# Scales from maxima, disjoint places, deferred loads and smaller pieces in a spectral feed-forward kernel

## The chip, the cores and the metric

The kernel runs on one core of one Trainium2 chip. The metric is the device time of one execution in microseconds (us), lower is better. Before the change it is 1247.22 us, the median of three runs (1246.28 to 1248.51). A core has five engines that work through their own instruction queues in order and wait for each other through semaphores: TensorE (PE in the profile; PEld is its loading of weights), VectorE (DVE), ScalarE (ACT), GpSimd (POOL) and SyncE (SP). DMAs are issued from the queues of SP, ACT and POOL, and stand in order with what else these queues hold.

## The reference

Inputs: x (2048 x 1024), complex filter weights w_r and w_i (2048 x 513), w1 (1024 x 3584) and w2 (3584 x 1024).

```
xn = layernorm(x)
s  = irfft2(rfft2(xn) * (w_r + 1j * w_i))
g  = silu(silu(xn @ w1) @ w2)
out = x + s * g
```

## The kernel before

**Precision.** Every matrix operand is split into two fp16 numbers, a high and a low part, scaled by powers of two; a product is three matmuls (high by high, high by low, low by high). A split costs one ScalarE activation (the high part, `high`, L232) and one VectorE operation (the low part, `low`, L235).

**First product.** xn is kept transposed in four row blocks c of 512 rows. w1 is taken in 28 column blocks f of 128. One call of `mm1(c, f)` is 24 matmuls (L454) into one of four PSUM tiles of the tag "ff"; there are 112 such calls. ScalarE applies the SiLU on evacuation (L463) into h32, and `hidden` forms differences (L492 to L497), splits them and stores them in DRAM over GpSimd's queue (L486).

**Scales of w1.** `weights1` loads a block (L252, SP's queue, buffers of the tag "w1"), and `maxi` gives one number for each partition: for blocks 0 to 3 the largest absolute value by VectorE (L256), for the others the sum of squares by ScalarE (L258), whose elementwise result is not needed and is written into place 3 of the tile scr. `scales` adds the numbers over the partitions with a matmul by ones into an "ff" tile (L239) and takes a power of two (L267 to L276). Then come the splits.

**Transform.** `fd_gen` does the forward transform of a row block: `fa_mat` (L769 to L771, 24 small products into one of two PSUM tiles of the tag "ft"), `fa_evac` (L777, L778 on ScalarE), butterflies on VectorE (L788 to L833), then a stage over rows with VectorE (L867, `radix4` at L219 to L222, L851), ScalarE (L848) and a store over GpSimd's queue (L852). After it `f_gen` applies the filter (matmuls at L975), and `i_gen` does the inverse for the row blocks in the order 1, 3, 0, 2 (`mat`, L1258; `mat2`, L1300; `bfly`). `load_i` (L1234) loads the operand zt of `mat`: 2 MB for a row block, from DRAM; for the three later row blocks it is called in the inverse of the block before, after its fourth `mat`. A small copy (L1244, ScalarE) writes one column into zt before `mat`.

**Maxima of filter and w2.** `wmax_gen` goes through the filter in 16 row blocks: two loads (L893, SP's queue, buffers "x", four of them), a maximum on VectorE (L898), and copies of its columns in another order on ScalarE (L901, L903) into two of the four places of scr, from which GpSimd's queue stores them to DRAM (L905). A block is used three steps after its load. `w2max_gen` does the like with 28 row blocks of w2: a load (L359), sums and differences on VectorE into places 0 to 2 in turn (L364), stored over GpSimd's queue (L365), and a sum of absolute values on ScalarE (L371), with place 3 for the unused result.

**Second product.** It is a product of 2 x 2 blocks with seven multiplications. Each of the seven has eight output groups j; one `mm2` is 42 matmuls of 512 columns (L532 to L534). The operand of the hidden layer is loaded again (ht, L513, SP's queue), two products ahead; the weights come through GpSimd's queue (L400) and are split on the way. Partial sums are read and written (pl, pd), and the last products apply the SiLU (L613), multiply by the transform's rows (L606), add x (L607) and store the output (L609). The very last one is done in two halves of 256 columns.

**Order.** Nothing is reordered by a compiler: the order in which the program emits instructions is the order on each engine. After each product `after` runs: `settle` gives out the next stage of the evacuation, `tick` runs what was deferred (`defer(n, fn)` runs fn n ticks later), and `work` gives out one step of the list wq (w1, later w2), one step of the list xq (filter maxima, then w2 maxima) and up to three steps of the list bg (layernorm, transform, inverse). The bg steps are paced by two sums of estimated costs, kept for every emitted instruction of VectorE and TensorE:

```
COST = {"DVE": ("dve", 0.07, 1.045e-3), "PE": ("pe", 0.0025, 0.4167e-3)}
...
clock["dve"] = max(clock["dve"], clock["pe"] - 1.0)
for _ in range(3):
    if clock["dve"] > clock["pe"] + lead[0] or hold[0] or slot(bg) == PAUSE:
        break
```

with a lead of 1 us (2 us in `f_gen`). The inverse's steps on bg wait for nothing else; `f_gen` starts when the xq list is done.

Of the kernel before, what the change touches and what calls it, by code (L numbers as in the profile page):

```python
# [10 lines left out]
F32 = mybir.dt.float32  # L11
# [13 lines left out]
SUMMED = (4, 5)  # L25
TURNED = (2, 3)
AT = (1, 0)
EXTRA = (4, 5, 6, 7, 20, 22, 24)


# [75 lines left out]
def spectral_ffn(ctx, tc, x, w_r, w_i, w1, w2, ca, kc, ci, tw, pm, out):  # L106
    nc = tc.nc
# [15 lines left out]
    pf = ctx.enter_context(tc.tile_pool(name="pf", bufs=4, space=PSUM))  # L123
# [28 lines left out]
    def defer(n, fn):  # L152
        deferred.append([n, fn])
# [74 lines left out]
    w2m = small("w2m", NFT)  # L228
# [13 lines left out]
    def weights1():  # L242

        raw = {}

        def load(i):  # L250
            raw[i] = fp.tile([128, 8, 128], F32, name=f"w1r{i}", tag="w1", bufs=7)
            nc.sync.dma_start(raw[i], w1v[:, :, i * 128:(i + 1) * 128])  # L252

        def maxi(i):
            if i < 4:
                nc.vector.tensor_reduce(m1[:, i:i + 1], raw[i], axis=AX.XY, op=OP.max, apply_absolute_value=True)  # L256
            else:
                nc.scalar.activation(A["scr"][:, 3].bitcast(mybir.dt.bfloat16), raw[i].rearrange("a b c -> a (b c)"), AF.Square, accum_out=m1[:, i:i + 1])  # L258

        def scales(i, k):  # L260
            sl = slice(i, i + k)
            ps = column_sums(f"s1_{i}", m1[:, sl], k)
            if i < 4:
                nc.vector.tensor_single_scalar(e1[:, sl].bitcast(I32), ps.bitcast(I32), 0x7F800000, op=OP.bitwise_and)
                nc.vector.tensor_single_scalar(e1[:, sl], e1[:, sl], 2.0**-100, op=OP.max)
            else:
                nc.vector.tensor_scalar(e1[:, sl].bitcast(I32), ps.bitcast(I32), 1, 0x7F800000, op0=OP.logical_shift_right, op1=OP.bitwise_and)  # L267
                nc.vector.tensor_scalar(e1[:, sl], e1[:, sl], 2.0**63, 2.0**-60, op0=OP.mult, op1=OP.max)
            nc.vector.reciprocal(r1[:, sl], e1[:, sl])
            nc.vector.tensor_single_scalar(rs[:, sl], r1[:, sl], 2.0**14, op=OP.mult)  # L270
            nc.vector.tensor_single_scalar(s1[:, sl], e1[:, sl], 2.0**-24, op=OP.mult)
            if (i + k) % 2 == 0:
                p = (i + k) // 2 - 1
                nc.vector.tensor_tensor(ep[:, p:p + 1], e1[:, 2 * p:2 * p + 1], e1[:, 2 * p + 1:2 * p + 2], op=OP.max)
                nc.vector.tensor_tensor(hs[:, p:p + 1], r1[:, 2 * p:2 * p + 1], r1[:, 2 * p + 1:2 * p + 2], op=OP.min)
                nc.vector.tensor_single_scalar(hs[:, p:p + 1], hs[:, p:p + 1], 2.0**7, op=OP.mult)  # L276

        new = {}

        def split(i):  # L280
            new[i] = fp.tile([128, 2, 8, 128], F16, name=f"w1_{i}", tag="w1", bufs=7)
            high(new[i][:, 0], raw[i], rs[:, i:i + 1])

        def rest(i):
            w1t[i] = w = new.pop(i)
            low(w[:, 1], raw.pop(i), rs[:, i:i + 1], w[:, 0])

        for i in range(4):
            load(i)
        yield 0  # L290
        maxi(0)
        yield 0
        maxi(1)
        yield 0
        scales(0, 2)
        yield 0
        split(0)
        rest(0)
        yield 0
        split(1)  # L300
        rest(1)
        maxi(2)
        maxi(3)
        yield 0
        scales(2, 2)
        split(2)
        rest(2)
        yield 2
        split(3)
        rest(3)  # L310
        yield 2
        def ahead(i):

            if i < NFT and i not in raw and i - len(used1) <= 4:
                load(i)
                load(i + 1)

        last = None
        for i in range(4, NFT, 2):
            while i not in raw:  # L320
                ahead(i)
                yield 0
                if last is not None:
                    rest(last)
                    last = None
            maxi(i)
            if last is not None:
                rest(last)
            yield 0
            maxi(i + 1)  # L330
            yield 0
            ahead(i + 2)
            yield 0
            ahead(i + 2)
            yield 0
            scales(i, 2)
            yield 0.8
            split(i)
            ahead(i + 2)
            yield 0.2  # L340
            rest(i)
            split(i + 1)
            ahead(i + 2)
            yield 0.2
            last = i + 1
        rest(last)
# [3 lines left out]
    def w2max_gen():  # L350

        ap = A["p"]
        scr = A["scr"]
        junk, slots = scr[:, 3].bitcast(F16), [0]
        tiles = {}
        for i in range(NFT + 3):
            if i < NFT:
                tiles[i] = ap.tile([128, 1024], F32, name=f"w2m{i}", tag="x", bufs=4)
                nc.sync.dma_start(tiles[i], w2[i * 128:(i + 1) * 128, :])  # L359
            if 3 <= i <= NFT + 2:  # L360
                def both(m, x0, x1, op):
                    d = scr[:, slots[0] % 3]
                    slots[0] += 1
                    nc.vector.tensor_tensor(d, x0, x1, op=op)  # L364
                    defer(1, lambda q=(i - 3) // 2: stores[0].dma_start(ws[m][q], d))  # L365

                t_ = tiles.pop(i - 3)
                if i % 2:
                    both(0, t_[:, 0:512], tiles[i - 2][:, 512:1024], OP.subtract)
                both(1 + i % 2, t_[:, 0:512], t_[:, 512:1024], OP.add)  # L370
                nc.scalar.activation(junk, t_, AF.Abs, accum_out=w2m[:, i - 3:i - 2])  # L371
            yield 0.7
        nc.vector.tensor_reduce(w2x, w2m, axis=AX.X, op=OP.max)
# [510 lines left out]
    def wmax_gen():  # L884

        ap = A["p"]
        scr = A["scr"]
        tl = {}
        for k in range(19):
            if k < 16:  # L890
                tl[k] = ap.tile([128, 2, 512], F32, name=f"wm{k}", tag="x", bufs=4)
                for i in range(2):
                    nc.sync.dma_start(tl[k][:, i], (w_r, w_i)[i][128 * k:128 * k + 128, 0:512])  # L893
            if k % 2:
                yield 0
            if k >= 3:
                t_, o = tl.pop(k - 3), scr[:, (slice(0, 2), slice(2, None, -2), slice(1, 3))[k % 3]]
                nc.vector.tensor_reduce(mt[:, k - 3:k - 2], t_, axis=AX.XY, op=OP.max, apply_absolute_value=True)  # L898
                src = t_.rearrange("m r (i l) -> m r l i", l=16)
                dst = o.rearrange("m r (g l i) -> m r l g i", g=4, l=4)  # L900
                nc.scalar.activation(o.rearrange("m r (l i) -> m r l i", i=32)[:, :, 0:4], src[:, :, 0:13:4], AF.Copy)  # L901
                for n, (la, st) in enumerate(((3, -1), (13, 1), (5, 1), (11, -1))):
                    nc.scalar.activation(dst[:, :, n, 1:4], src[:, :, la:la + 3 * st:st], AF.Copy)  # L903
                for i in range(2):
                    defer(1, lambda o=o, i=i, k=k: stores[0].dma_start(wp[i][128 * k - 384:128 * k - 256, :], o[:, i]))  # L905
            yield 1.1
# [329 lines left out]
    def i_gen(c):  # L1236
# [114 lines left out]
        for i in range(6):  # L1351
            if i < 4:
                mat(i)
            if i >= 2:
                split(i - 2)
            if 1 <= i <= 4:
                post(i - 1)
            yield PAUSE if i in (1, 2) else 3.9 if i in (3, 4) else 2
        if c != IORDER[-1]:
            n = IORDER[IORDER.index(c) + 1]  # L1360
            open_zt(n)
            load_i(n)
            load_kk(n)
        yield PAUSE
        for p in range(5):
            if p < 4:
                mat2(p)
            if p:
                bfly(p - 1)
            yield 3.4 if p else 0.3  # L1370
# [41 lines left out]
    with tc.manual_schedule():  # L1412
# [138 lines left out]
        for n, (m, j) in enumerate(seq):  # L1551
# [2 lines left out]
                    load_h(*seq[n + 2], k)  # L1554
            if n == len(seq) - 1:
                load_parts(m, j)
                for b in range(2):
                    cols = slice(256 * b, 256 * b + 256)
                    ps = pf.tile([128, 256], F32, name=f"pb{m}_{j}_{b}", tag="ff")
                    for k in range(2):  # L1560
                        mm2(m, j, ps, k, cols)
                    for _ in range(4 * b):
                        settle()
                        tick()
                    after(acc(m, j, ps, cols))
                break
# [54 lines left out]
```

## Time and profile before

| | |
|---|---|
| median of three runs | 1247.22 us (1246.28 to 1248.51) |
| the profiled execution, its own time | 1245.75 us |
| its span, first to last instruction | 1244.0 us |
| TensorE busy | 1209.3 us (97%) |
| VectorE busy | 1008.0 us (81%) |
| ScalarE busy | 524.2 us (42%) |
| GpSimd busy | 372.1 us (30%) |
| mean DMA rate over the span | 244 GB/s |

In a line of the profile, L454 is line 454 of the kernel, "pa<-xnT,w" says which tile is written from which, "x24" counts instructions, and in a timeline the bracket gives the idle time of the engine just before, and what ended it ("issue" where the profile shows nothing waited for). A wait for several semaphores is put down to the one that came last. Times are us from the span's start.

### The profile page before, as it was taken

Reading aid. Unit: us, or ns where it says so; the run is one execution under the profiler, and the core shown is the slowest. Engines: PE = TensorE matmul, PEld = TensorE weight load, DVE = VectorE, ACT = ScalarE, POOL = GpSimd, SP = SyncE. Lnnn points to the kernel's source line nnn. Section 1 sums busy time; section 2 is a strip of 40 time slices with the busy share of each in tenths; the row PEclk is TensorE's granted clock in tenths of the full one; section 3 lists DMA queues with packets and bytes.
Section 4 is the critical chain, followed back from the end, with each engine's and each line's share of the span. In section 5 each row is a group of like instructions: output and inputs, shape, how many; then the busy total and the mean of one; then the engine's idle time right before and its main releaser. Section 6 shows DMA issues by size and latency. Waiting matters only on the chain.

```text
span 1244.0 us, 21981 instructions
## 1 busy us (share of the span) xinstructions
PE 1209.3 (97%) x8335; PEld 602.4 (48%) x8335; DVE 1008.0 (81%) x2043; ACT 524.2 (42%) x716; POOL 372.1 (30%) x585
## 2 busy tenths in 40 slices
PE   7999999969999989999999999999999999999998
PEld 5544454435454434454444445445545544444544
DVE  6678998979989887549987998993876959779964
ACT  4865456847665565434444232121222212233221
POOL 1241153444453235313453224721212121010000
PEclk9999999999999999999999999999999999999999
DMA  7478477667687889565797989987877999994897
GB/s 239 124 177 200 127 257 226 211 221 222 227 300 226 280 280 292 173 189 153 218 319 217 295 240 273 275 252 215 213 235 220 272 341 298 288 390 176 274 372 264
DMA packets 170474, 303.79 MB, mean 244 GB/s; under 512 B 33584, under 2 KB 86480, under 8 KB 170368
## 3 DMA queue, kind: packets, MB, share of 16 engines
q1 hardware_dynamic: 131408, 183.48, 47.5%
q0 software_dynamic: 38816, 118.78, 31.7%
q8 instruction: 65, 1.06, 0.3%
q14 instruction: 41, 0.34, 0.1%
q10 hardware_dynamic: 144, 0.13, 0.0%
HBM read 185.39 MB, written 112.74 MB: 240 GB/s over the span
## 4 chain that ended last, share of the span: by engine, by line
PE 65%; DVE 6%; DMA 4%; ACT 1%; issue 1%; POOL 0%; SPq 0%; DVEq 0%; ACTq 0%; POOLq 0%
PE pa L454 22%; PE pb L532 13%; PE pb L534 12%; PE pb L533 12%; PE fx L975 2%; DMA ht<-hd_one 2%; PE iu L1258 1%; PE id L1300 1%; DMA vd<-Rs 1%; DMA ws<-scr 1%; DVE pl L606 0%; DVE scr L364 0%; DMA kv<-vd 0%; DVE hoone L235 0%; DVE us L1288 0%
## 5 line engine op out<-in xcount | busy, mean ns | idle before, releaser
L454 PE MATMUL pa<-xnT,w 128*128 128x512 f16 x2688 | 588.3, 380 | 7.1 <-ACT h L463 4.2
L454 PEld LDWEIGHTS <-w 128*128 128x128 f16 x2688 | 262.8, 98 | 320.8 <-issue 10.2
L532 PE MATMUL pb<-w,ht 128*128 128x512 f16 (+1 forms) x798 | 299.8, 376 | 1.8 <-DMA ht<-hd_one 1.8
L534 PE MATMUL pb<-w,ht 128*128 128x512 f16 (+1 forms) x798 | 299.5, 375 | 0.0
L533 PE MATMUL pb<-w,ht 128*128 128x512 f16 (+1 forms) x798 | 299.5, 375 | 0.0
L532 PEld LDWEIGHTS <-ht 128*128 128x128 f16 x798 | 78.0, 98 | 92.5 <-DMA ht<-hd_one 2.0
L534 PEld LDWEIGHTS <-ht 128*128 128x128 f16 x798 | 78.1, 98 | 91.2
L533 PEld LDWEIGHTS <-ht 128*128 128x128 f16 x798 | 78.1, 98 | 87.2
L463 ACT ACTIVATE h<-pa,s 128x512 f32<-128x512 f32 x112 | 75.7, 678 | 65.1 <-PE pa L454 57.9
L400 POOL DMA_DIRECT2D jr<-in_B_w_dram x56 | 35.2, 636 | 165.9 <-DVE w L235 47.4
L486 POOL DMA_DIRECT2D hd_sum<-hosum x52 | 38.5, 778 | 153.2 <-DVE hosum L235 77.6
L232 ACT ACTIVATE w<-jr,sc 128x512 f16<-128x512 f32 x98 | 67.9, 712 | 30.2 <-PE pb L534 16.3
L235 DVE SCALAR_TENSOR_TENSOR hoone<-h,hs,hoone 128x2048 f16<-128x2048 f32 x28 | 65.6, 2344 | 12.4 <-ACT hoone L232 6.6
L235 DVE SCALAR_TENSOR_TENSOR w<-jr,sc,w 128x512 f16<-128x512 f32 x98 | 71.6, 745 | 0.0
L232 ACT ACTIVATE hoone<-h,hs 128x2048 f16<-128x2048 f32 x28 | 55.9, 1996 | 28.2 <-DMA hd_one<-hoone 20.1
L492 DVE TENSOR_TENSOR hr<-h 128x1024 f32<-128x1024 f32 x28 | 34.2, 1220 | 35.2 <-ACT h L463 35.0
L486 POOL DMA_DIRECT2D hd_one<-hoone x52 | 46.1, 886 | 52.3 <-DVE hoone L235 29.7
L232 ACT ACTIVATE hosum<-hr,hs 128x1536 f16<-128x1536 f32 x28 | 44.0, 1572 | 41.5 <-DVE hr L493 35.5
L613 ACT ACTIVATE pl<-pl,c 128x512 f32<-128x512 f32 (+1 forms) x26 | 16.9, 683 | 102.0 <-DVE pl L592 53.3
L232 ACT ACTIVATE w<-w1r,rs 128x1024 f16<-128x1024 f32 x28 | 31.8, 1144 | 49.8 <-DVE w L235 37.7
L235 DVE SCALAR_TENSOR_TENSOR hosum<-hr,hs,hosum 128x1536 f16<-128x1536 f32 x28 | 50.7, 1812 | 1.1 <-ACT hosum L232 1.1
L365 POOL DMA_DIRECT2D ws<-scr x42 | 27.7, 678 | 51.7 <-DVE scr L364 42.5
(234 smaller groups left out, 1748.3 us busy)
## 6 DMA issues: line engine op xcount, KB each, us to landing
jr<-in_B_w_dram POOLq DMA_DIRECT2D x84, 256.0 KB, 7.2
w1r<-in_B_w_dram SPq DMA_DIRECT2D x28, 512.0 KB, 6.0
w2m<-in_B_w_dram SPq DMA_DIRECT2D x28, 512.0 KB, 6.5
ht<-hd_dif SPq DMA_DIRECT2D x32, 448.0 KB, 7.3
ht<-hd_sum SPq DMA_DIRECT2D x32, 448.0 KB, 5.7
ht<-hd_one SPq DMA_DIRECT2D x32, 448.0 KB, 8.2
hd_sum<-hosum POOLq DMA_DIRECT2D x52, 256.0 KB, 3.4
hd_one<-hoone POOLq DMA_DIRECT2D x52, 256.0 KB, 5.2
```

Source lines behind the costliest of these rows:

```text
L232: nc.scalar.activation(hi, raw, AF.Copy, scale=scale)
L235: nc.vector.scalar_tensor_tensor(lo, raw, scale, hi, op0=OP.mult, op1=OP.subtract)
L365: defer(1, lambda q=(i - 3) // 2: stores[0].dma_start(ws[m][q], d))
L400: nc.gpsimd.dma_start(raw[n], ws[m][q] if m in ws else w2_block(m, q, 0))
L454: nc.tensor.matmul(ps, w[:, wh, d], xt[:, xh, d], start=(n == 0), stop=(n == 23))
L463: nc.scalar.activation(hq[:, 2 * (c % 2) + f % 2], ps, AF.Silu, scale=s1[:, f:f + 1])
L486: defer(1, lambda k=k, m=m: stores[0].dma_start(hd[m, g][:, :, q].rearrange("f p h s -> f p (h s)"), o[:, k].rearrange("f p h s -> f p (h ...
L492: tt(sums[:, 0:2], hq[:, 0::2], hq[:, 1::2], op=OP.subtract)
L532: nc.tensor.matmul(ps, hh[:, 0], w[:, 0], start=first, stop=False)
L533: nc.tensor.matmul(ps, hh[:, 0], w[:, 1], start=False, stop=False)
L534: nc.tensor.matmul(ps, hh[:, 1], w[:, 0], start=False, stop=last)
L975: nc.tensor.matmul(o, k[rows_, h, e + 2 * x, kh, kind], B["v"][u, h][rows_, e + 2 * x, vh, cols], start=(n == 0 and kind == 1), stop=(n == ...
```

## The change

Five edits. (1) The column blocks 10 to 15 of w1 get their scale from the maximum on VectorE, as blocks 0 to 3 did; the sums of squares on ScalarE remain for the rest. (2) `wmax_gen` writes into places 0 and 1 and places 2 and 3 of scr in turn, in place of the three pairs (0, 1), (2, 0), (1, 2). (3) The loads of `wmax_gen` and `w2max_gen` are deferred by one tick. (4) For the three later row blocks of the inverse, `load_i` loads a quarter of zt at the old place and one more in each of the next three steps, ahead of the first three `mat2`. (5) The very last product is done in parts of 256, 128 and 128 columns.

```diff
+PEAKS = (0, 1, 2, 3, 10, 11, 12, 13, 14, 15)
...
         def maxi(i):
-            if i < 4:
+            if i in PEAKS:
...
         def scales(i, k):
...
-            if i < 4:
+            if i in PEAKS:
...
     def w2max_gen():
...
+        def load(i):
+            tiles[i] = ap.tile([128, 1024], F32, name=f"w2m{i}", tag="x", bufs=4)
+            nc.sync.dma_start(tiles[i], w2[i * 128:(i + 1) * 128, :])
+
         for i in range(NFT + 3):
             if i < NFT:
-                tiles[i] = ap.tile([128, 1024], F32, name=f"w2m{i}", tag="x", bufs=4)
-                nc.sync.dma_start(tiles[i], w2[i * 128:(i + 1) * 128, :])
+                defer(1, lambda i=i: load(i))
...
     def wmax_gen():
...
+        def load(k):
+            tl[k] = ap.tile([128, 2, 512], F32, name=f"wm{k}", tag="x", bufs=4)
+            for i in range(2):
+                nc.sync.dma_start(tl[k][:, i], (w_r, w_i)[i][128 * k:128 * k + 128, 0:512])
+
         for k in range(19):
             if k < 16:
-                tl[k] = ap.tile([128, 2, 512], F32, name=f"wm{k}", tag="x", bufs=4)
-                for i in range(2):
-                    nc.sync.dma_start(tl[k][:, i], (w_r, w_i)[i][128 * k:128 * k + 128, 0:512])
+                defer(1, lambda k=k: load(k))
...
-                t_, o = tl.pop(k - 3), scr[:, (slice(0, 2), slice(2, None, -2), slice(1, 3))[k % 3]]
+                t_, o = tl.pop(k - 3), scr[:, 2 * (k % 2):2 * (k % 2) + 2]
...
     def i_gen(c):
...
+        n = None
         if c != IORDER[-1]:
             n = IORDER[IORDER.index(c) + 1]
             open_zt(n)
-            load_i(n)
+            load_i(n, (0,))
             load_kk(n)
         yield PAUSE
         for p in range(5):
+            if n is not None and p < 3:
+                load_i(n, (p + 1,))
             if p < 4:
                 mat2(p)
...
             if n == len(seq) - 1:
                 load_parts(m, j)
-                for b in range(2):
-                    cols = slice(256 * b, 256 * b + 256)
-                    ps = pf.tile([128, 256], F32, name=f"pb{m}_{j}_{b}", tag="ff")
+                for b, cols in enumerate((slice(0, 256), slice(256, 384), slice(384, 512))):
+                    ps = pf.tile([128, cols.stop - cols.start], F32, name=f"pb{m}_{j}_{b}", tag="ff")
                     for k in range(2):
                         mm2(m, j, ps, k, cols)
-                    for _ in range(4 * b):
+                    for _ in range(4 if b else 0):
```

## The prediction

> **What bounds the kernel now.** I read first the page's busy times, then what TensorE waited for, then the windows around those waits. From the page, with shares of the span:
>
> ```profile
> span 1244.0 us, 21981 instructions
> ...
> PE 1209.3 (97%) x8335; PEld 602.4 (48%) x8335; DVE 1008.0 (81%) x2043; ACT 524.2 (42%) x716; POOL 372.1 (30%) x585
> ```
>
> TensorE is the bound nearly everywhere: it is idle for only 34.7 us (1244.0 less 1209.3). The view of waits, for PE alone (total, times, longest), shows the pieces that matter here:
>
> ```profile
> PE fa L769 <- ACT L L778: 11.3, 1, 11.3
> PE pa L454 <- ACT h L463: 4.2, 1, 4.2
> ...
> PE pb L532 <- DMA ht<-hd_one: 1.8, 1, 1.8
> ```
>
> The windows (length; busy time of PE, PEld, DVE, ACT, POOL with counts; granted clock; DMA share; GB/s) place the first two:
>
> ```profile
> 250.00:275.00 25.00, 19.57 (x128) 10.41 (x127) 16.79 (x28) 10.56 (x14) 10.24 (x16) 0.97 0.67 229
> 275.00:300.00 25.00, 19.15 (x118) 10.82 (x118) 23.95 (x59) 20.57 (x37) 11.70 (x18) 0.82 0.63 201
> 300.00:325.00 25.00, 25.00 (x119) 11.49 (x117) 24.58 (x62) 13.33 (x21) 11.40 (x18) 1.00 0.70 231
> ...
> 450.00:475.00 25.00, 20.84 (x87) 9.00 (x86) 20.75 (x33) 15.14 (x22) 10.55 (x16) 0.86 0.91 313
> ```
>
> Each stall also costs granted clock (0.82, 0.86), and VectorE is almost full (24.58 of 25) after the first: between 250 and 475 us two engines have to be watched.
>
> **The first stall** is TensorE waiting for ScalarE to empty a PSUM tile of the forward transform (L777, L778). ScalarE's timeline tells why it came late:
>
> ```profile
> 250.15 0.66 ACT L463 ACTIVATE h<-pa,s 128x512 f32<-128x512 f32 x1
> 264.94 0.63 ACT L901 ACTIVATE scr<-wm 128x256 f32<-128x256 f32 x1 [14.14 <-issue]
> ...
> 279.73 0.60 ACT L777 ACTIVATE L<-fa 128x520 f32<-128x520 f32 x1
> ```
>
> L901 writes reordered filter columns into scr. The pairs used in turn (0 and 1, 2 and 0, 1 and 2) each share a place with the pair before, so a write waits until the previous store has landed. GpSimd's timeline shows that store issued late, and the view of scr from 200 to 300 us gives the landing:
>
> ```profile
> 242.83 1.08 POOL L905 DMA_DIRECT2D wp<-scr  x2 [3.56 <-ACT scr L903]
> ...
> 258.46 1.57 POOL L905 DMA_DIRECT2D wp<-scr  x2
> ```
>
> ```profile
> DMA to landing us min/median/max: 2.3/5.1/6.5
> ```
>
> 258.46 plus 6.5 is 264.96, which is when L901 starts. The price on TensorE: the idle time, and half a clock after it.
>
> ```profile
> 262.89 0.22 PE L769 MATMUL fa<-cas,xnT 128*128 128x128 f16 x1
> ...
> 264.23 5.34 PE L454 MATMUL pa<-xnT,w 128*128 128x512 f16 x24
> ...
> 280.85 0.27 PE L769 MATMUL fa<-cas,xnT 128*128 128x128 f16 x1 [11.28 <-ACT L L778]
> ...
> 283.36 5.64 PE L454 MATMUL pa<-xnT,w 128*128 128x512 f16 x24
> ```
>
> The 24 transform matmuls take 2.51 us after the stall (280.85 to 283.36) against 1.34 (262.89 to 264.23), the next 24 take 5.64 against 5.34: 1.47 lost, 12.75 with the idle time.
>
> **The second stall** has another root. VectorE waited, from 250 to 467 us (total, times, longest), for:
>
> ```profile
> DVE scr L364 <- DMA ws<-scr: 13.5, 7, 5.2
> DVE Rs L851 <- ACT Rs L848: 8.5, 3, 7.8
> DVE e L267 <- PE s L239: 1.5, 1, 1.5
> DVE hr L492 <- ACT h L463: 0.7, 1, 0.7
> ```
>
> The 7.8 us is the first stall seen from VectorE (L848 stands behind L901 in ScalarE's order). The 13.5 us are waits for the stores of the w2 sums, and they leave VectorE late, ScalarE behind it, and TensorE without a free accumulator:
>
> ```profile
> 466.29 1.01 PE L454 MATMUL pa<-xnT,w 128*128 128x512 f16 x2 [4.17 <-ACT h L463]
> ```
>
> ```profile
> 466.00:474.40 8.40, 8.11 (x26) 3.10 (x26) 8.30 (x14) 4.01 (x7) 7.04 (x11) 0.66 0.79 246
> ```
>
> 26 matmuls take 8.11 us here; at 5.34 for 24 they would take 5.79: 2.3 us of clock, 6.5 with the idle time.
>
> **The change, part by part.** *Two disjoint pairs of places.* A write then waits for the store two back. For the write at 264.94 that is the one issued at 242.83 and landed by 249.4, so ScalarE goes on at 250.8: its 14.14 us and VectorE's 7.8 us are gone. How much of 12.75 us reaches the end? VectorE decides. From 260 to 466 us it is the chain that TensorE meets at the second stall, and of its waits the change takes 7.8, and the two on TensorE (1.5 and 0.7) go because TensorE is now ahead: 10.0 us. The 13.5 us on the w2 stores stay, since those use three places in turn as before. TensorE comes 12.75 us earlier to the second stall and is let go 10.0 us earlier; the stall grows to 4.17 + 12.75 - 10.0 = 6.9 us, or about 3 us of it stay at 269 us, since ScalarE reaches L777 only when VectorE lets it (279.73 less 7.8 is 271.9, where TensorE is at 269.2). I take -10.0; bounds -4.9 (a write still waits once for a whole median landing, 5.1) and -12.75 - 6.5 = -19.3 (VectorE catches up and both stalls go).
>
> *Six maxima.* Blocks 10 to 15 leave ScalarE's squares, which write place 3, now used by the second pair, for VectorE's reduction. The nearest row has the same 1024 elements:
>
> ```profile
> L898 DVE TENSOR_REDUCE mw<-wm 128x1 f32<-128x1024 f32 x16 | 19.4, 1211 | 0.0
> ```
>
> Six by 1.21 is 7.3 us on an engine with 0.4 us free in 300 to 325. What hides it: the order of work adds up a cost for every VectorE instruction and gives out background work (the transform) only while that sum is within 1 us of TensorE's. The six count in it, so 7 us of background go out later, past 466 us, into VectorE's slack there. So 0; bounds 0 and +7.3, if that cover fails. The scales keep their number of small operations. One wait is new: the matmul that sums the maxima over the partitions (L239) now waits for VectorE, with all of TensorE behind it; it comes three products, 16 us, after the second maximum is given out, and VectorE has at times waited for that matmul (the 1.5 us), so I cost it at nothing. ScalarE's relief is not on the path.
>
> *Loads one turn later.* In SP's queue a deferred load comes ahead of the next turn's w1 load, as it did; on the w2 side it waits for VectorE anyway (the view of waits for SP, 300 to 480 us):
>
> ```profile
> SPq L359 <- DVE scr L364: 109.0, 20, 15.3
> ```
>
> So 0; bounds -6.5 (the second stall, the only place where it could help) and +6.5, one such load late by a whole landing. From the page (KB each, us to landing):
>
> ```profile
> w2m<-in_B_w_dram SPq DMA_DIRECT2D x28, 512.0 KB, 6.5
> ...
> zt<-zd SPq DMA_DIRECT2D x6, 1024.0 KB, 13.7
> ```
>
> *Inverse operand in four pieces.* For each of the three later row blocks, two zt loads of 1024 KB become eight of 256 KB; six of them go out over the next three turns. The chain of waits shows the load that TensorE misses for 1.8 us, and the timelines of SP and ScalarE the zt loads ahead of it and the copy that completes the operand:
>
> ```profile
> 1061.00 19.43 DMA ht<-hd_one
> ```
>
> ```profile
> 1058.90 1.33 SPq L1234 DMA_DIRECT2D zt<-zd  x2
> ```
>
> ```profile
> 1104.79 0.26 ACT L1244 ACTIVATE zt<-zpp 128x16 f16<-128x16 f16 x1
> ```
>
> The window over that load (the DMA engines all busy, 256 GB/s):
>
> ```profile
> 1058.00:1082.00 24.00, 21.64 (x266) 12.09 (x264) 18.37 (x48) 3.56 (x6) 2.15 (x4) 1.00 1.00 256
> ```
>
> With 1.5 of the 2 MB moved behind it, at 256 GB/s the ht load lands about 6 us earlier, and the 1.8 us go. The pieces now also stand in SP's queue behind the stores of finished rows, which wait for VectorE; the ht loads stand behind the pieces. The copy comes 46 us after the loads, so even a piece that is 30 us later is there; if one were not, ScalarE's evacuations would stand behind the copy. -1.8; bounds -1.8 and +2 (a later ht load meets one piece pair, 0.5 MB, ahead of it).
>
> *Last product in three.* From the last accumulator to the last sum VectorE needs 2.78 us now (1238.39 to 1241.17):
>
> ```profile
> 1238.39 0.41 DVE L592 TENSOR_TENSOR pl<-pl,pb 128x256 f32<-128x256 f32 x1
> ...
> 1240.75 0.42 DVE L607 TENSOR_TENSOR pl<-pl,fx 128x256 f32<-128x256 f32 x1
> ```
>
> ```profile
> L607 DVE TENSOR_TENSOR pl<-pl,fx 128x256 f32<-128x256 f32 x4 | 1.7, 424 | 0.1
> ...
> L1332 DVE TENSOR_TENSOR so<-sab 128x128 f32<-128x128 f32 x4 | 1.2, 292 | 0.1
> ```
>
> Half the width saves 0.13 us on each of five VectorE steps and about as much on one of ScalarE: 0.76. The matmuls of a quarter go at 1.34/24 = 56 ns, 84 of them 4.7 us; 42 of a half go at 4.68/43 = 109 ns, 4.6 us:
>
> ```profile
> 1233.10:1238.00 4.90, 4.68 (x43) 3.94 (x41) 4.66 (x9) 0.91 (x2) 0.00 (x0) 1.00 0.25 92
> ```
>
> So -0.6; bounds -0.9 and +0.3 (narrower output rows landing more slowly, which no row shows).
>
> The Trainium skill speaks against this edit: "TensorE: Matmul & The Clock Gate", "Back-to-back issue gap", gives about 81 ns for each load and matmul of 128 columns in a real stream. By it the 84 would take an estimated 6.8 us, the edit cost 1.5 and the sum below be -10.3. The trace's own stream of the same shape, weights loaded each time, has 56 ns, and I go by that.
>
> **Sum.** -10.0 + 0 + 0 - 1.8 - 0.6 = -12.4. The profiled execution took 1245.75 us (1.75 around its span), so 1233.3; the median of the runs shown, 1247.22, lies 1.47 above it: 1234.8.
>
> **Rivals.**
> - *The maxima eat the gain* (18%). The transform's background work is what ScalarE and VectorE are late with at 466 us, so putting it off helps nothing and the 7.3 us stand in the chain: -10.0 + 7.3 - 2.4 = -5.1, 1242.1. For it: 24.58 of 25. Against: less transform is then in front of the same product.
> - *Both stalls go* (15%): -19.3 - 2.4 = -21.7, 1225.5. For it: with ScalarE not held, GpSimd's queue also moves earlier. Against: 13.5 us of waits that no edit touches.
>   The same page, under "HAM oscillation", puts the loss of clock at idle gaps over about 3.4 us; the 4.17 us stall agrees. If the second were kept shorter than that, its 2.3 us would be saved as well, 1232.5 in place of 1234.8.
> - *The stall only moves* (9%): the store two back is late too, because GpSimd's queue, not the number of places, sets it; ScalarE waits one write later. Then only 2.4 go: 1244.8. Against: the store at 242.83 left the moment its columns were written (GpSimd had waited 3.56 us for them).
> - *Slower* (5%): ScalarE's wait moves as in the last and the maxima are not covered: +7.3 - 2.4 = +4.9, 1252. It decides if VectorE's waits on L848 stay above some 5 us while the six reductions stand ahead of the same products.
>
> **Numbers.** My forecast has 53%. Its own spread is about 5 us either way (part of the waits on late stores, the +2 of the ht loads). From 1227 to 1243 lie it, the first rival and the near side of the second; about 2 in 10 stay outside. A measurement of this kernel tells 0.2% (2.5 us) from no change: faster than 1244.7 are the forecast, the first two rivals and 2 of the third's 9, 88%; within 0.2%, 6 of those 9; slower, the last rival and the rest, 6%.
>
> **What would show it.** In the waits for PE the 11.3 us line on L769 gone or under 6; no wait of L901 over 3 us; VectorE's 7.8 us on L848 gone; the wait on L364 still 10 to 16 us and PE's wait on L463 between 400 and 480 us at 3 to 8 us (gone: the second rival); VectorE's busy time up by 7.3 and ScalarE's squares 24 down to 18; no PE wait on ht<-hd_one; the last L592 to the last L607 in about 2.0 us. What would make it wrong: a new PE wait after 280 us, since 7 us of background work now meets other turns, or a product waiting for scales whose maximum VectorE has not reached.

## The result, and the profile after

The changed kernel takes 1229.32 us, the median of four runs (1226.38 to 1231.56), against 1247.33 us for the kernel before (1246.28 to 1248.51, four runs beside it). The ratio is 0.9854, 95% interval [0.9831, 0.9877]: 18.0 us less, where the prediction had 12.4. Measured once more, with other runs of the kernel before beside it, it had 1230.39 and a ratio of 0.9862 [0.9836, 0.9888]. The profiled execution took 1228.6 us.

Busy times, from the page of the changed kernel:

```profile
span 1226.8 us, 22097 instructions
...
PE 1206.8 (98%) x8377; PEld 602.4 (49%) x8377; DVE 1016.0 (83%) x2055; ACT 517.5 (42%) x706; POOL 365.7 (30%) x585
```

VectorE is 8.0 us busier than before, ScalarE 6.7 less. The groups of VectorE and of ScalarE (count; busy, mean ns of one; idle time before) show the six blocks that moved, 4 to 10 maxima at the duration foreseen, and 24 to 18 squares:

```profile
L257 DVE TENSOR_REDUCE m<-w1r 128x1 f32<-128x1024 f32 x10 | 12.0, 1213 | 0.0
```

```profile
L259 ACT ACTIVATE scr<-w1r 128x1024 bf16<-128x1024 f32 x18 | 18.9, 1052 | 16.8 <-DMA w1r<-in_B_w_dram 16.8
```

TensorE's idle time is 20.0 us, where it was 34.7. What TensorE waited for (total, times, longest); these two rows are the largest behind 100 us:

```profile
PE fx L984 <- DMA kv<-vd: 1.8, 1, 1.8
...
PE fa L774 <- ACT L L783: 1.5, 1, 1.5
```

The 11.3 us on the transform's tile (now L774 <- L783), the 4.2 us on the accumulator (L463, now L468) and the 1.8 us on ht are all gone; one wait of 1.5 us on the transform's tile stands at 393 us. Between 247 and 272 us ScalarE's writes of filter columns into scr, one of which had 14.14 us of idle time before it, have no bracket:

```profile
248.99 0.63 ACT L910 ACTIVATE scr<-wm 128x256 f32<-128x256 f32 x1
...
267.89 0.63 ACT L910 ACTIVATE scr<-wm 128x256 f32<-128x256 f32 x1
```

The windows (length; busy time of PE, PEld, DVE, ACT, POOL with counts; granted clock; DMA share; GB/s) that answer to those of before, the last one 18 us earlier:

```profile
250.00:275.00 25.00, 25.00 (x119) 11.54 (x118) 24.77 (x40) 15.59 (x24) 15.74 (x24) 1.00 0.72 224
275.00:300.00 25.00, 25.00 (x172) 13.68 (x171) 21.96 (x40) 18.36 (x29) 14.91 (x24) 1.00 0.99 311
300.00:325.00 25.00, 25.00 (x135) 12.08 (x134) 24.73 (x70) 15.03 (x25) 8.66 (x13) 1.00 0.64 195
432.00:457.00 25.00, 25.00 (x119) 11.49 (x118) 22.96 (x51) 15.70 (x24) 8.32 (x13) 1.00 0.83 290
```

TensorE is busy throughout in all four, at full clock. VectorE's waits from 250 to 467 us:

```profile
DVE scr L369 <- DMA ws<-scr: 4.4, 3, 2.4
DVE e L265 <- PE s L240: 2.6, 1, 2.6
DVE Rs L856 <- ACT Rs L853: 2.0, 1, 2.0
```

The wait on L848 (now L853) fell from 8.5 to 2.0 us, as foreseen. But the 13.5 us on the stores of the w2 sums, which the prediction left standing, are 4.4, and the 1.5 us on the matmul of the sums (L239, now L240), which it had going away, are 2.6.

To see where the time went I followed the start of every product (the first of its 24 matmuls of L454) through both traces, with both set to zero at product 40, which starts ahead of the first stall:

| part of the span | difference, us |
|---|---|
| start-up, to product 40 (half a clock from 11.5 to 14.9 us after the change) | +1.09 |
| first stall, products 42 to 50 | -12.92 |
| products 58 to 76 (the wait at 393 us) | +1.64 |
| second stall, products 76 to 78 | -6.95 |
| products 92 to 94 (first filter load) | +0.58 |
| wait for ht | -1.86 |
| from there to the end (last product) | +1.25 |
| span | -17.17 |

So both stalls went in full, and two small items were lost again. Between products 43 and 50 the background work stands at other turns, so the split inside the first row is not meaningful, its total is.

### The profile page after: what moved, and what is told of

Read it like the earlier page. It is cut to its first block, busy times and chain, and to the rows that moved or that the text cites. A ratio compares the mean times of both kernels' runs of the same rounds, so it can differ in the third digit from the quotient of the medians.

```text
span 1226.8 us, 22097 instructions
## 1 busy us (share of the span) xinstructions
PE 1206.8 (98%) x8377; PEld 602.4 (49%) x8377; DVE 1016.0 (83%) x2055; ACT 517.5 (42%) x706; POOL 365.7 (30%) x585
## 4 chain that ended last, share of the span: by engine, by line
PE 80%; DVE 9%; DMA 4%; ACT 3%; issue 3%; POOL 1%; SPq 0%; DVEq 0%; ACTq 0%; POOLq 0%
PE pa L459 37%; PE pb L537 12%; PE pb L538 12%; PE pb L539 12%; PE fx L984 2%; DMA fx<-in_A_x_dram 2%; PE id L1309 1%; PE iu L1267 1%; DVE w L236 1%; ACT xp L701 1%; PE tp L710 1%; DMA w1r<-in_B_w_dram 1%; DVE hoone L236 0%; DVE pl L611 0%; DMA x<-in_A_x_dram 0%
## 5 line engine op out<-in xcount | busy, mean ns | idle before, releaser
L537 PE MATMUL pb<-w,ht 128*128 128x512 f16 (+2 forms) x812 | 300.7, 372 | 0.0
L538 PE MATMUL pb<-w,ht 128*128 128x512 f16 (+2 forms) x812 | 300.4, 372 | 0.0
L539 PE MATMUL pb<-w,ht 128*128 128x512 f16 (+2 forms) x812 | 300.3, 372 | 0.0
L539 PEld LDWEIGHTS <-ht 128*128 128x128 f16 x812 | 79.4, 98 | 91.0
L537 PEld LDWEIGHTS <-ht 128*128 128x128 f16 x812 | 79.4, 98 | 90.5
L538 PEld LDWEIGHTS <-ht 128*128 128x128 f16 x812 | 79.5, 98 | 87.2
L468 ACT ACTIVATE h<-pa,s 128x512 f32<-128x512 f32 x112 | 75.5, 677 | 58.4 <-PE pa L459 51.4
L618 ACT ACTIVATE pl<-pl,c 128x512 f32<-128x512 f32 (+2 forms) x28 | 17.5, 656 | 97.2 <-DVE pl L597 54.1
L1023 POOL DMA_DIRECT2D zd<-zq x32 | 28.2, 927 | 51.7 <-DVE zq L1018 39.0
```

The lines of the kernel that those rows point to most:

```text
L468: nc.scalar.activation(hq[:, 2 * (c % 2) + f % 2], ps, AF.Silu, scale=s1[:, f:f + 1])
L537: nc.tensor.matmul(ps, hh[:, 0], w[:, 0], start=first, stop=False)
L538: nc.tensor.matmul(ps, hh[:, 0], w[:, 1], start=False, stop=False)
L539: nc.tensor.matmul(ps, hh[:, 1], w[:, 0], start=False, stop=last)
L1023: defer(1, lambda h=h, to=to: stores[0].dma_start(to, t_[64 * h:64 * h + 64]))
```

## The experiments

The prediction's account (A) is that the disjoint pairs take the first stall away, while VectorE's waits on the w2 stores keep a second. Two rivals were put beside it: the order of the background work, which the counted maxima shift, takes the second stall away (B); or the pairs alone free both (C). The next table has, for each kernel's profiled execution, the start of a product against the kernel before, both again zero at product 40. The column "second stall" is the step from product 76 to 78. Each run has its own section below, in this order: order_only is the kernel before with the new order alone, maxima_only the kernel before with the six maxima, the two pairs kernels are the changed kernel with hardly any maxima (uncounted in the old order, counted in the new one), uncounted is all of the change in the old order, undo_loads the change without the deferred loads, and vd_scalar pairs_uncounted with the transform's stores in another queue.

| kernel | at product 50 | second stall | last matmul | median us | ratio to before |
|---|---|---|---|---|---|
| changed kernel | -12.92 | -6.95 | -19.34 | 1229.32 | 0.9854 |
| order_only | +2.37 | -6.96 | -0.20 | 1240.49 | 0.9947 |
| maxima_only | +0.14 | -6.96 | -7.40 | 1241.36 | 0.9956 |
| pairs_uncounted | -8.56 | +0.37 | -10.11 | 1234.01 | 0.9903 |
| uncounted | -6.37 | -2.15 | -8.11 | 1238.86 | 0.9938 |
| pairs_counted | -12.91 | -6.96 | -19.84 | 1228.27 | 0.9855 |
| undo_loads | -12.92 | -6.96 | -16.93 | 1229.92 | 0.9868 |
| vd_scalar | -12.91 | -1.02 | -15.09 | 1230.54 | 0.9873 |

### The order of the background work, without any other change

```
 accum_out=m1[:, i:i + 1])
+if 10 <= i < 16:
+    clock["dve"] += (0.07 + 1.045e-3 * 1024) * pace[0]
```

> The kernel before, with one line more: for the column blocks 10 to 15 the cost of a maximum (1.14 us each) is added to VectorE's sum of estimated costs, though the squares stay on ScalarE. No instruction is added, removed or changed; only the background work is given out later, as in the changed kernel. Three accounts of why the second stall (4.17 us idle and 2.3 us of clock at 466 us) went together with the first. A, the prediction's: the stores of the w2 sums set it, and nothing but the first stall's 10 us moves: here no change, 1247.3, with 11.3 us on the transform's tile and 4.2 us at 466 us as before. B, the order: background work one turn later is what takes VectorE's waits on the w2 stores away (13.5 us before, 4.4 after): here the second stall goes and the first stays, 1247.3 - 6.5 = 1240.8. C, the pairs: ScalarE not being held at 250 us frees GpSimd's queue and with it the stores: here no change, 1247.3. A and C differ in the runs with the pairs.

Measured: 1240.49 (1236.46 to 1245.57, ten runs), ratio 0.9947 [0.9930, 0.9964]: 6.35 us faster with not one instruction added or taken. TensorE's and VectorE's waits (the latter from 250 to 467 us) in the profiled execution, which was the slowest of the ten:

```profile
PE fa L771 <- ACT L L780: 11.8, 2, 10.2
...
PE pb L534 <- DMA ht<-hd_one: 2.4, 1, 2.4
PE pa L456 <- ACT h L465: 2.0, 2, 1.1
```

```profile
DVE scr L366 <- DMA ws<-scr: 7.5, 6, 2.3
```

The first stall is there as before, the waits on the w2 stores are nearly halved, and no wait on the accumulator over 1.1 us is left: the second stall went, by 6.96 us in the table. That is B, to the number (1240.8). In this execution the gain is used up elsewhere (2.4 us later at the first stall, 1.8 us more by product 76), so its last matmul is only 0.20 us earlier; the 6.35 us are the difference of the medians. It says that what I had counted as cover, at zero, is a gain of its own.

### The six maxima alone

```
+PEAKS = (0, 1, 2, 3, 10, 11, 12, 13, 14, 15)
...
-            if i < 4:
+            if i in PEAKS:
```

> The kernel before with the six maxima on VectorE alone (they count in the sum of costs); pairs, loads, pieces and halves as before. Prediction's account (A): the 7.3 us of VectorE are covered by background work that moves behind them, first stall as before, 1247.3, second stall 4 us. If they are not covered: 1247.3 + 7.3 = 1254.6, with the second stall at 4.2 + 7 = 11 us. B, the order: as the run with the order alone, 1240.8. C, the pairs: 1247.3.

Measured: 1241.36 (1237.85 to 1242.43), ratio 0.9956 [0.9940, 0.9973]. The same as the order alone, though VectorE does the 7.3 us of reductions here. By the medians they are covered. The ht wait is gone here too, without the pieces; more on that below.

### The pairs, with hardly any maxima, in the old order

```
-nc.vector.tensor_reduce(m1[:, i:i + 1], raw[i], ...)
+was = clock["dve"]
+nc.vector.tensor_reduce(m1[:, i:i + 1], raw[i] if i < 4 else raw[i][:, 0:1, 0:8], ...)
+if i >= 4:
+    clock["dve"] = was + 0.0
```

> The changed kernel, but for the column blocks 10 to 15 the maximum is taken over 8 of the 1024 elements of each partition (most of that maximum is left out), and it does not count in the sum of costs. So the background work has the order of the kernel before and VectorE next to no new work: the disjoint pairs, with squares off place 3, act by themselves, beside the loads, the pieces and the three parts. A, the prediction's: only the first stall goes, VectorE still waits some 13 us for the w2 stores, the second stall is 3 to 7 us idle: 1234.8. B, the order: the second stall stays at 4 us or more idle and 2.3 us of clock: 1229.3 + 6.5 = 1235.8. C, the pairs: both stalls go, 1229.3.

Measured: 1234.01 (1232.65 to 1236.05), ratio 0.9903 [0.9886, 0.9921]. This is A's number (1234.8) and B's (1235.8); C is out. What TensorE and then ScalarE (240 to 300 us) and VectorE (250 to 467 us) waited for:

```profile
PE pa L462 <- ACT h L471: 4.9, 1, 4.9
PE fa L777 <- ACT L L786: 2.7, 1, 2.7
```

```profile
ACT Rs L856 <- DMA vd<-Rs: 9.1, 2, 6.1
```

```profile
DVE scr L372 <- DMA ws<-scr: 13.8, 7, 5.4
```

In the old order the pairs do in outline what the prediction says of them, with both its alternatives at once: 2.7 us of the first stall stay near 270 us, and the second is 4.9 us. The w2 waits are 13.8 us, as foreseen. What it had not seen is the row for ScalarE. The wait of L901 on the wp store is gone, but the next store wait in the same stretch comes up in its place: ScalarE now waits 6.1 us for a transform store (vd<-Rs) before it may write Rs again. In the changed kernel's order that row does not occur.

### The pairs in the new order, still with hardly any maxima

```
-    clock["dve"] = was + 0.0
+    clock["dve"] = was + (0.07 + 1.045e-3 * 1024) * pace[0]
```

> As the run before (maximum over 8 of 1024 elements for the blocks 10 to 15, most of it left out), but each counts in the sum of costs as if it were the whole: order of the background work as in the changed kernel, without the 7.3 us of VectorE. A, the prediction's, with the maxima covered: 1229.3, like the changed kernel. If the maxima cost something in the changed kernel after all: faster by that, down to 1222. B, the order: 1229.3. C, the pairs: 1229.3, and the run without the count the same.

Measured: 1228.27 (1226.7 to 1229.4), ratio 0.9855 [0.9838, 0.9872], against 1234.01 with only the count different: the order is worth 5.7 us on top of the pairs, where it was worth 6.35 without them. And against the changed kernel's 0.9854 and 0.9862 the six whole maxima cost nothing that can be measured, though this kernel's VectorE is busy 1009.4 us against 1016.0.

### All of the change, in the old order

```
+was = clock["dve"]
 nc.vector.tensor_reduce(m1[:, i:i + 1], raw[i], ...)
+if i >= 4:
+    clock["dve"] = was
```

> The changed kernel with all its parts, but the six maxima do not count in the sum of costs: the background work keeps the order of the kernel before, and the 7.3 us of VectorE come on top. A, the prediction's: the cover is gone, 1229.3 + 7.3 = 1236.6, and VectorE waits 10 to 16 us for the stores of the w2 sums. B, the order: the second stall is back, with the 7.3 us in it: 1229.3 + 6.5 + 0 to 7.3 = 1235.8 to 1243. C, the pairs: no second stall even so if the maxima fit into waits that are gone: 1229.3, at most a few us more.

Measured: 1238.86 (1237.87 to 1240.68), ratio 0.9938 [0.9919, 0.9957]. That is 9.5 us slower than the changed kernel, within B's bounds, and by the medians 4.9 us slower than the same order with small maxima (4.4 by the ratios, which is the better comparison, since the two ran on different chips). So uncovered, the reductions seem to cost some 4 to 5 of their 7.3 us. The profiled executions do not show it: the whole maxima lose 2.2 us at the first stall (-6.37 against -8.56) and win 2.5 back at the second. Of the 2.0 us that they are behind at the last matmul, 1.6 are a half-clock stretch at 762 us that no wait precedes, and the rest is a wait for ht.

### The loads at once

```
-                defer(1, lambda i=i: load(i))
+                load(i)
...
-                defer(1, lambda k=k: load(k))
+                load(k)
```

> The changed kernel with the loads of the filter blocks and of w2 given out at once, not one turn later. Prediction's account: the order of SP's queue is the same with and without the delay, so 1229.3, within 1 us. Rival: the later load is what sets free VectorE's waits on the w2 stores, because the two share the DMA engines: then the second stall is back, 1229.3 + 6.5 = 1235.8.

Measured: 1229.92 (1229.61 to 1231.97), ratio 0.9868 [0.9850, 0.9887]. Nothing, as predicted.

### The transform's stores in another queue

In the old order two stores vd<-Rs are issued at products 73.6 and 75.6, just ahead of the second stall (73.6 is six tenths of the way through product 73); in the new order none is issued between products 65 and 77. GpSimd's timeline of the kernel before:

```profile
444.09 1.04 POOL L852 DMA_DIRECT2D vd<-Rs  x1
...
454.43 0.72 POOL L852 DMA_DIRECT2D vd<-Rs  x1 [1.97 <-DMA vd<-Rs]
```

This run asks whether GpSimd's queue is the way in which the order acts. It starts from pairs_uncounted.

```
-defer(2, lambda: stores[0].dma_start(vd[j][:, :, c], sp[j]))
+defer(2, lambda: (nc.scalar if stores[0] is nc.gpsimd else stores[0]).dma_start(vd[j][:, :, c], sp[j]))
```

> As the run with pairs_uncounted (maximum over 8 of 1024 elements for the blocks 10 to 15, most of it left out, and not counted, so the background order of the kernel before), but the stores of the transform's rows (vd<-Rs) go out over ScalarE's queue, not GpSimd's. In the old order two of them stand in GpSimd's queue among the products 73 to 76, just ahead of the second stall, and the store of a w2 sum there leaves 4.4 to 5.0 us after its sum is written; in the new order none stands there and it leaves after 2.2 us. If these stores in GpSimd's queue are the way in which the order acts: VectorE's waits on the w2 stores fall from 13.8 us to some 7, PE's 4.9 us wait on the accumulator at the second stall goes, 1234.0 - 6 = 1228. If the order acts by VectorE's and ScalarE's own row-stage work standing ahead of the product (three places for the sums, whatever the queue): no change, 1234, the waits still 12 to 14 us.

Measured: 1230.54 (1229.6 to 1231.91), ratio 0.9873 [0.9854, 0.9893]. Between the two expectations, and the trace says why. What TensorE, ScalarE (240 to 300 us) and VectorE (250 to 467 us) waited for:

```profile
PE pa L462 <- ACT h L471: 2.9, 1, 2.9
```

```profile
ACT Rs L856 <- DMA vd<-Rs: 1.5, 1, 1.5
```

```profile
DVE scr L372 <- DMA ws<-scr: 16.0, 8, 5.4
```

At the first stall the queue is the cause: ScalarE's 6.1 us wait is gone, TensorE's 2.7 us with it, and product 50 comes 12.91 us earlier, as in the new order. At the second it is not: the w2 waits are still there (16.0 us), and TensorE still waits for the accumulator. It is let go 6.0 us earlier than in pairs_uncounted, but it also gets there 4 us earlier. TensorE's timeline, first of pairs_uncounted and then of this run:

```profile
457.76 10.43 PE L462 MATMUL pa<-xnT,w 128*128 128x512 f16 x37 [4.90 <-ACT h L471]
```

```profile
451.76 16.41 PE L462 MATMUL pa<-xnT,w 128*128 128x512 f16 x62 [2.93 <-ACT h L471]
```

That the new order takes the second stall away is shown in all five of its rows of the table (-6.95 or -6.96). By which step, the waits on the w2 stores or the transform's row stage on VectorE and ScalarE standing behind product 77 and not ahead of it, no run separates, and I leave it open.

### The operand whole, and the last product in halves

```
-            load_i(n, (0,))
+            load_i(n)
...
-            if n is not None and p < 3:
+            if False:
```

> The changed kernel with the inverse's operand loaded whole at the old place, as before. Prediction's account: TensorE's wait of 1.8 us for ht is back: 1231.1. Rival: the pieces cost elsewhere what they save: 1229.3.

Measured: 1231.09 (1229.09 to 1232.01), ratio 0.9876 [0.9859, 0.9894], which the changed kernel's two measurements overlap. The views of tile ht around its load say how long it took, first with the operand whole and then in the changed kernel:

```profile
DMA to landing us min/median/max: 17.5/17.7/17.9
```

```profile
DMA to landing us min/median/max: 8.4/9.0/9.6
```

The pieces halve the landing in these two executions. But with the operand whole it is 17.7 us here, against 19.7 in the kernel before, and that is enough: no matmul shows a wait for ht. This is one execution, though, and at 1229.09 us the fastest of its four; the others took 1230.22 to 1232.01, and whether they waited is not known. With the operand whole the wait is 1.8 us in the kernel before, 2.4 in order_only and nil in maxima_only; with the pieces it is still 0.5 in undo_loads and 0.4 in uncounted. So the pieces take away a wait of some 2 us that is there in some executions and not in others, and whether the other edits had already removed it here stays open.

```
-for b, cols in enumerate((slice(0, 256), slice(256, 384), slice(384, 512))):
+for b, cols in enumerate((slice(0, 256), slice(256, 512))):
```

> The changed kernel with the last product in two halves of 256 columns, as before. Prediction's account: 0.6 us slower, 1229.9. What the trace of the changed kernel suggests: it is faster without it by about 1.1 us, 1228.2, since from the last matmul's end to the end of the span there are 7.32 us with three parts against 6.22 before; VectorE, with more and smaller steps, is what is late there.

Measured: 1226.45 (1224.96 to 1229.01), ratio 0.9844 [0.9825, 0.9864]. The medians alone (2.9 us) are within their spread, but the traces are steady: from the last matmul's end to the last sum on VectorE it takes 4.45 or 4.46 us with three parts (in all eight profiled executions that have them) and 3.39 or 3.40 with two (in all six). The three parts cost about 1.1 us there. VectorE's timeline at the end, three parts:

```profile
1219.64 0.42 DVE L612 TENSOR_TENSOR pl<-pl,fx 128x256 f32<-128x256 f32 x1
1219.99 0.28 DVE L597 TENSOR_TENSOR pl<-pl,pb 128x128 f32<-128x128 f32 x1
...
1221.71 0.29 DVE L612 TENSOR_TENSOR pl<-pl,fx 128x128 f32<-128x128 f32 x1
1221.92 0.28 DVE L597 TENSOR_TENSOR pl<-pl,pb 128x128 f32<-128x128 f32 x1
...
1223.64 0.29 DVE L612 TENSOR_TENSOR pl<-pl,fx 128x128 f32<-128x128 f32 x1
```

and in the kernel before, the step just ahead of the L592 at 1238.39:

```profile
1238.05 0.43 DVE L607 TENSOR_TENSOR pl<-pl,fx 128x256 f32<-128x256 f32 x1
```

No L597 has a bracket: VectorE came to each straight from the step before. The last matmul had ended at 1219.48. The two quarters take 3.94 us on VectorE one after the other (1219.99 to 1223.93), the one half took 2.78. The last quarter alone takes the 2.0 us that the prediction gave as a sign (1221.92 to 1223.93), but VectorE comes to it late, from the quarter before.

### Further in the same direction

```
+if i >= 4:
+    clock["dve"] += (0.07 + 1.045e-3 * 1024) * pace[0]
```

> The changed kernel with the last product in two halves as before, and the six maxima counted twice in the sum of costs, so that the background work goes out a further step later in places. If later is better because VectorE is then less loaded ahead of 466 us: a little faster than the halves alone, 1224 to 1226. If the gain of the order is only where single steps happen to fall: anything from 1222 to 1240, with stalls at other products.

Measured: 1227.07 (1225.63 to 1228.76), ratio 0.9845 [0.9825, 0.9866], no different from the halves alone. The gain does not grow with the count.

The changed kernel as it is, on the same chip:

> The changed kernel itself, unchanged, for the comparison on the same chip: 1229.3, ratio to the kernel before 0.985 to 0.986.

Measured: 1230.39 (1226.84 to 1231.71). The profiled executions of the changed kernel (spans of 1226.8 and 1229.9 us) differ by the wait at 393 us, 1.5 us in the first and 2.7 in the second, and by the half-clock stretches.

The last run puts together what had helped: halves, and the transform's stores on ScalarE's queue.

```
-for b, cols in enumerate((slice(0, 256), slice(256, 384), slice(384, 512))):
+for b, cols in enumerate((slice(0, 256), slice(256, 512))):
...
-            defer(2, lambda: stores[0].dma_start(vd[j][:, :, c], sp[j]))
+            defer(2, lambda: (nc.scalar if stores[0] is nc.gpsimd else stores[0]).dma_start(vd[j][:, :, c], sp[j]))
```

> The changed kernel, all maxima whole and counted, with the last product in two halves and the stores vd<-Rs over ScalarE's queue. If late stores in GpSimd's queue still cost something in the new order (the 1.5 to 2.9 us wait of TensorE on the transform's tile near 393 us): 1224 to 1225. If that wait comes from elsewhere (the column blocks of w1 landing late for ScalarE's squares): as the halves alone, 1226.5. If ScalarE's added issues (0.52 us each on its queue) make it late: 1227 to 1230.

Measured: 1224.24 (1224.04 to 1226.13), ratio 0.9824 [0.9805, 0.9843]. It is the fastest of all: 5 to 6 us under the changed kernel by medians, 3.7 to 4.7 by the ratios. Against the halves alone (0.9844, product 76 at -9.99) the intervals overlap, so what the stores' queue adds rests on the trace. Product 76 comes 12.91 us earlier than in the kernel before, as product 50 does, so that what the changed kernel loses in between (1.64 us, and 4.5 in its second profile) is not lost here; the wait on L774 <- L783 near 393 us is gone.

## Why the prediction was right or wrong

**The forecast and its luck.** The measured 1229.32 is 5.5 us from my 1234.8 and 3.8 us from the 1225.5 of the rival "both stalls go", and by the sign that I gave for it (TensorE's wait on the accumulator gone) it is that rival. That the number is no further off is partly luck, since errors offset each other: the stalls and what lies between them gave 8.2 us more than the term, the last product took 1.85 us more than its term, and 1.67 us were lost where no step had any.

**First stall: cause right, size of the term off.** L901's wait on the wp store set it: with the maxima and the new order but the old pairs (maxima_only) the stall stays, with the pairs it goes, with the deferred loads and without them (undo_loads). The term -10.0 came from the chain through VectorE. In the old order the pairs kernel (pairs_uncounted) gained 8.56 us there and lost 0.37 at the second stall, so the path held in outline and the size was 2 us too good: ScalarE's 6.1 us on the transform's store, behind the same queue, is what I had not looked for. It is a partial form of the rival "the stall only moves". The waits that made up the 10.0 did not go as listed. Of the 8.5 us on L848 (7.8 in one piece), 3.8 are left in that run. The 1.5 us on the matmul of the sums grew to 2.2 there and 2.6 in the changed kernel. The 0.7 us went, but its row is a wait on ScalarE, not on TensorE. And TensorE ran dry at 269.57 us by the rows shown (264.23 plus 5.34), not at 269.2, so the alternative leaves 2.3 us of the stall, not 3; 2.7 were measured.

**"The 13.5 us on the w2 stores stay": the step that failed.** They are 4.4 and 7.9 us in the two profiles of the changed kernel, and the stall that was to grow to 6.9 us is nil. The rival "both stalls go" had 15% because "no edit touches" those waits. One did: the count of the maxima in the sum of costs. The rival's own reason, GpSimd's queue moving earlier once ScalarE is not held, is not the cause: in pairs_uncounted ScalarE is not held on scr, and the second stall stays.

**Six maxima at 0: right, and the medians agree with the reason.** Without the cover they cost some 4 to 5 us by medians (uncounted against pairs_uncounted; the traces do not show where), with it nothing that can be measured. But I priced the shift of 7 us of background work only as cover. By itself it is worth 6.35 us without the pairs, and 5.7 with them. "Putting it off helps nothing", in the first rival, is refuted by the run with the order alone. The new wait on L240 never held TensorE.

**Loads at 0: right**, 1229.92 without that edit.

**Pieces at -1.8: the load moved as worked out, whose gain it is stays open.** I had ht landing about 6 us earlier; it was 8.7 (17.7 to 9.0). The term is in the trace (-1.86), but the same wait is also gone in the one profiled execution with the operand whole.

**Last product at -0.6: wrong in sign, some +1.1** (+1.25 in the table's last row, which begins at the wait for ht). The step that failed is the saving of "half the width on each of five VectorE steps". It took the last accumulator as what VectorE waited for. The quoted row for L592 had no bracket, so VectorE was behind already, and the steps of both quarters count: 3.94 us against 2.78, since a step of half the width takes 0.28 us and not half of 0.41. The bound of +0.3 was too narrow for the same reason. The matmuls went as I had them: 84 in 1214.63 to 1219.26, 56 ns each. The Trainium skill's 81 ns ("TensorE: Matmul & The Clock Gate", "Back-to-back issue gap") does not fit this stream; its sign for the edit came true by another mechanism, on VectorE.

**The sum.** -10.0 where -18.23 was measured (-12.92 + 1.64 - 6.95), -1.8 and -1.86, -0.6 and +1.25, and +1.67 for the start and the filter's load, which no step had.

## What to carry to other kernels

Where a cost model hands out the order of work, an edit that changes a cost changes the order, and that can be worth as much as the edit: run the order alone, with the cost added and nothing else. When a wait on a store is removed, look for the next store wait of the same engine and queue, since it was hidden behind the first. Before a last piece is split to shorten its tail, look whether the engine was idle just ahead of it; if its row has no idle bracket, more pieces can be only more steps, as they were here.

## What the runs showed of the hardware

The half-clock stretches of TensorE lie on a fixed grid. In the fourteen profiles of this case every one between 100 us and the tail lasts 3.41, 6.83 or 10.24 us, and two of one execution start a whole number of 3.413 us apart (273.72 and 464.86 us in the kernel before: 56.0 times). Cutting TensorE's timeline into cells of that grid, a cell at full clock with 1.94 us of idle or more was always followed by a half-clock cell, one with 1.69 us or less was not, but for the exception below; between these both occur. The windows over such a cell and the next, first of undo_loads, then of undo_thirds (the last product in halves):

```profile
390.60:394.00 3.40, 1.48 (x26) 1.39 (x25) 2.88 (x14) 3.40 (x6) 0.00 (x0) 0.99 1.02 405
394.00:397.40 3.40, 3.40 (x11) 1.16 (x9) 0.89 (x2) 2.74 (x6) 0.00 (x0) 0.50 0.80 322
```

```profile
388.80:392.20 3.40, 1.47 (x7) 0.59 (x6) 3.37 (x17) 2.49 (x5) 0.00 (x0) 1.00 1.09 381
392.20:395.60 3.40, 2.57 (x30) 1.93 (x30) 1.68 (x6) 3.40 (x5) 0.00 (x0) 1.00 1.02 415
```

In the first kernel one wait of 1.9 us is followed by a whole cell at half clock, an estimated 1.7 us more: from product 50 to 76 it loses 3.76 us. In the second a wait of 2.76 us, which the grid splits into 1.93 and 0.83, costs no clock: over the same products it loses 2.92. The Trainium skill ("TensorE: Matmul & The Clock Gate", "HAM oscillation") speaks of idle gaps over about 3.4 us; the prediction took that for the length of a gap, and here some 1.9 us within one cell were enough, so a stall's price in clock depends on where it falls. The exception: three executions (of undo_pieces, which loads the operand whole, of uncounted, and of after_again, the changed kernel once more) have a half-clock cell at 753 to 762 us with no wait over 0.4 us before it, beside the small matmuls of the filter (L984); what makes it I do not know.
